# Grouped-query attention on one core: 120 score columns of every ninth chunk exponentiated on VectorE, PV three chunks behind, V spreads retimed

## The chip, the cores and the metric

One core of a Trainium2 chip. The metric is the device time of the whole program in microseconds, as a median of several executions. All executions used here count as fast ones; the granted TensorE clock is shown as 1.00 in the profiles, except where the text says otherwise.

## The reference

```python
# B, Hq, Hkv, Sq, Sk, D = 16, 32, 8, 288, 512, 128 ; bf16 ; q, k, v ~ 0.05 * normal
k = jnp.repeat(k, rep, axis=1)            # rep = 4 query heads per K/V head
v = jnp.repeat(v, rep, axis=1)
scores = jnp.einsum("bhqd,bhkd->bhqk", q, k) * D ** -0.5
p = softmax(scores, axis=-1)
return jnp.einsum("bhqk,bhkd->bhqd", p, v)
```

There are 16 x 8 = 128 groups (one K/V head each). A group has 4 x 288 = 1152 query rows, that is nine tiles of 128, and is worked through in three chunks of three tiles. So there are 384 chunks. A chunk has 512 keys x 384 rows of scores; laid out with keys on the partitions that is a 128 x 1536 tile.

## The kernel before

For each chunk n, TensorE makes the scores (six matmuls, 1536 columns), ScalarE takes the exponential of all 1536 columns in one instruction straight out of PSUM, TensorE multiplies by V (12 matmuls of 129 columns; the 129th column of V is one and gives the row sums), and VectorE takes the reciprocal of the sums and scales the result out of PSUM. GpSimd spreads V into a layout with room for the column of ones. No maximum is subtracted; a check of the sums at the end falls back to a general path that never runs here.

```python
def op_s(n):                                   # scores of chunk n
    waits = [have("k", g), have_q(g, i)]
    if n >= 2:
        waits.append(("s_e", n - 1))           # exponential n-2 is done: two score buffers
    for x, (c, j, r0, w) in enumerate(pieces): # 384,128,256,256,128,384 columns
        ... matmul(ps_s[:, n % 2, c:c + w], kt_sb[:, sl, j, gi, :], qg[:, r0:r0 + w])

def op_exp(n):                                 # ScalarE
    waits = [("s_s", n + 1)]
    if n >= NPT:                               # NPT = 4 probability buffers
        waits.insert(0, ("s_pv", n - NPT + 1))
    ... activation(pt_sb[:, n % NPT], ps_s[:, n % 2], Exp, scale=scale)

def op_pv(r):                                  # 12 matmuls into PSUM bank r % 2
    waits = [("s_vc", g + 1), ("s_e", r + 1)]
    if 2 <= r < NS - 1:
        waits.append(("s_ev", r - 1))          # eviction r-2 is done: two output banks

def op_vc(g):                                  # GpSimd spreads V of group g
    waits = [have("v", g)]                     # as soon as the load has landed
    if u >= NSLOT:
        waits.append(("s_pv", NC * (g - NSLOT * UG + 1)))
...
# TensorE's program                            # VectorE's program
for n in range(NS):                            # for r in range(NS - 1):
    op_s(n)                                    #     op_rc(r)   reciprocal
    if n >= LAG: op_pv(n - LAG)   # LAG = 2    #     op_ev(r)   eviction
```

Of the kernel before, what the change touches and what calls it, by code (L numbers as in the profile page):

```python
# [1 line left out]

# [118 lines left out]
    return {"pool": on_pool, "sp": on_sync, "pe": on_tensor, "dve": on_vector, "act": on_scalar}  # L121


def bass_standalone__gqa_softmax__near_ridge_kernel(
    nc: bass.Bass,
    q: bass.AP,
# [18 lines left out]
    assert COLS % CH == 0 and NT == NC * TPC and NJ * P == BANK  # L145
    scale = float(D) ** -0.5
    DV = D + 1
    VP = 160
    LAG = 2
    TW = TPC * P  # L150
    UG = 4
    NU = NG // UG
    NSLOT = 3
    NQ = 12
    NPT = 4
    WARM = 5
    AHEAD = 1.08
    NO = 12
    NS = NG * NC
# [10 lines left out]
    with ExitStack() as es:  # L170
# [14 lines left out]
            S("us_v%d" % i)  # L185
        for i in range(UG):
            S("s_k%d" % i)
        for name in ["s_v0", "s_v2", "s_s0", "s_kd0", "s_kd1", "s_id", "s_kp"]:
            S(name)
        for i in range(NQ):  # L190
            S("s_q%d" % i)
# [36 lines left out]
        st_sb = main.enter_context(nc.sbuf_tensor("st_sb", [P, 2, B], FP32))  # L228
        ck_sb = main.enter_context(nc.sbuf_tensor("ck_sb", [P, 3], FP32))
        bad_sb = main.enter_context(nc.sbuf_tensor("bad_sb", [P, 2, ALONE + 1], FP32))  # L230
        one_f = main.enter_context(nc.sbuf_tensor("one_f", [P, 1], FP32))
        z_sb = main.enter_context(nc.sbuf_tensor("z_sb", [P, BANK], BF16))
        dum = main.enter_context(nc.sbuf_tensor("dum", [P, 2], FP32))
# [15 lines left out]
        def emit(eng, waits, fn):  # L249
            waits = need(eng, waits)  # L250
            for (s, n) in waits[:-1]:
                eng.wait_ge(s, n)
            ins = fn()
            if waits:
                ins.wait_op(waits[-1][0], waits[-1][1], "sem-ge")
            return ins
# [95 lines left out]
        def op_s(n):  # L352
            eng = nc.tensor
            g, i = n // NC, n % NC
            sl, gi = (g // UG) % NSLOT, g % UG
            waits = [have("k", g), have_q(g, i)]
            if n >= 2:
                waits.append(("s_e", n - 1))
            qg = qt_sb[:, g % NQ, i * TPC:(i + 1) * TPC].rearrange("d t p -> d (t p)")
            for x, (c, j, r0, w) in enumerate(pieces):  # L360
                ins = emit(eng, waits if x == 0 else [], lambda: eng.matmul(  # L361
                    ps_s[:, n % 2, c:c + w], kt_sb[:, sl, j, gi, :], qg[:, r0:r0 + w], start=True, stop=True))
                if n == 0 and c + w == BANK:
                    ins.then_inc(sem["s_s0"], 1)
            ins.then_inc(sem["s_s"], 1)

        def outs(r):

# [4 lines left out]
        def op_pv(r):  # L373
            eng = nc.tensor
            g = r // NC
            sl, gi = (g // UG) % NSLOT, g % UG
            waits = [("s_vc", g + 1), ("s_e", r + 1)]
            if 2 <= r < NS - 1:
                waits.append(("s_ev", r - 1))


            for j in range(NJ):
                for a in range(TPC):
                    ins = emit(eng, waits if a == 0 and j == 0 else [], lambda: eng.matmul(  # L384
                        outs(r)[:, a, :], pt_sb[:, r % NPT, j, a * P:(a + 1) * P],
                        v_sb[:, sl, gi * NJ + j, 0:DV], start=(j == 0 and a == 0), stop=(j == NJ - 1),
                        skip_group_check=True))
            ins.then_inc(sem["s_pv"], 1)
# [13 lines left out]
        def op_exp(n):  # L402
            eng = nc.scalar
            waits = [("s_s", n + 1)]
            if n >= NPT:
                waits.insert(0, ("s_pv", n - NPT + 1))
            dst, src = pt_sb[:, n % NPT], ps_s[:, n % 2].rearrange("p (j r) -> p j r", r=TW)
            parts = [(dst.rearrange("p j r -> p (j r)"), ps_s[:, n % 2])]
            if n == 0:
                d, s = parts[0]  # L410
                emit(eng, [("s_s0", 1)], lambda: eng.activation(d[:, 0:BANK], s[:, 0:BANK], ACTF.Exp, scale=scale))  # L411
                parts = [(d[:, BANK:CH], s[:, BANK:CH])]
            if n == NS - 1:
                w = TW - P
                parts = [(dst[:, :, 0:w], src[:, :, 0:w]), (dst[:, :, w:TW], src[:, :, w:TW])]
            for (d, s) in parts:
                emit(eng, waits, lambda: eng.activation(d, s, ACTF.Exp, scale=scale)).then_inc(sem["s_e"], 1)  # L417


        def op_vc(g):  # L420
            eng = nc.gpsimd
            u, gi = g // UG, g % UG
            sl = u % NSLOT
            waits = [have("v", g)]
            if u >= NSLOT:
                waits.append(("s_pv", NC * (g - NSLOT * UG + 1)))
            emit(eng, waits, lambda: eng.tensor_copy(  # L427
                v_sb[:, sl, gi * NJ:(gi + 1) * NJ, 0:D], vd_sb[:, sl, gi].rearrange("p (j d) -> p j d", d=D))
            ).then_inc(sem["s_vc"], 1)
# [80 lines left out]
        @block.tensor  # L510
        def _(eng):
            op_warm(WARM, BANK, ps_o[:, 1])
            op_kt(0, range(NJ), 0)
            op_warm(6, P, ps_s[:, 1])
            for n in range(NS):
                if n == LAG:
                    op_kt(1, range(NJ), 1)
                    op_warm(4, P, ps_o[:, 0])
                op_s(n)
                if n >= LAG:  # L520
                    op_pv(n - LAG)
            for r in range(NS - LAG, NS - 1):
                op_pv(r)
            for a in range(TPC):
                op_pv_last(a)
            emit(eng, [("s_ev", NS - 1), ("s_bad", 2)], lambda: eng.matmul(  # L526
                ps_o[0:1, NS % 2, 0:ALONE + 1], one_f[:], bad_sb[:, 1, :], start=True, stop=True)
            ).then_inc(sem["s_bad"], 1)
            choose(eng, "pe")

        @block.scalar
        def _(eng):
            op_kd(eng, 0)
            emit(eng, [("s_one", 1)], lambda: eng.activation(dum[:, 1:2], dum[:, 0:1], ACTF.Exp))  # L534
            op_v(0, eng, 0, 2)
            op_kd(eng, 1)
            for n in range(NS):
                op_exp(n)
            op_ev_act()
            choose(eng, "act")  # L540
# [13 lines left out]
        def _(eng):  # L554
# [6 lines left out]
            w0 = NS - 1 - ALONE // TPC  # L561
            last = rl_sb[:, NG * NT - ALONE:NG * NT]
            for r in range(NS - 1):
                op_rc(r)
                op_ev(r)
                if r % per_b == per_b - 1 and r < NS - 1:
                    op_stat(r // per_b)
                if r == w0:
                    op_stat(B - 1)
                if r == w0 + 1:  # L570
                    emit(eng, [("s_stat", B)], lambda: eng.tensor_reduce(
                        ck_sb[:, 0:1], st_sb[:, 0, :], AX.X, ALU.max))
                    eng.tensor_reduce(ck_sb[:, 1:2], st_sb[:, 1, :], AX.X, ALU.min).then_inc(sem["s_stat"], 1)
                if r == w0 + 2:
                    op_over(ck_sb[:, 0:1], ck_sb[:, 1:2], ALONE, ALONE + 1, ("s_stat", B + 1), B + 2)
# [37 lines left out]
```

## Time and profile before

| | kernel before |
|---|---|
| median of 3 runs | 527.37 us (527.22 to 528.51) |
| span of the profiled run | 525.4 us |
| busy share TensorE, ScalarE, VectorE, GpSimd | 99, 99, 55, 14 % |
| score group to score group, first 30 chunks | 1.335 us |
| the same afterwards | 1.343 us |
| duration of one exponential as recorded | 1.46 us at the start, 1.76 us later |

The profile is of one execution. The views used in what follows: the page's busy times, the source view of one line (count, shortest/median/longest duration in ns, first and last start), the chain of waits (the work that ended last, in order of time), the table of waits, and the timeline. Two engines are shown as full, so the distance between the starts of one kind of instruction tells more than the busy share. The lines themselves are in the prediction below.

The *starts* of the first exponentials are 1.331 us apart but their *ends* 1.343, from the second chunk on: the recorded start of an instruction that sits behind another on ScalarE is not the start of its own work, and the growing duration is the difference. And TensorE's first score matmul of a chunk takes 0.163 us until the next in the first 30 chunks and 0.170 to 0.172 afterwards, which is the whole visible sign of its wait for ScalarE.

### The profile page before, as it was taken

The page shows a single profiled execution, that of the slowest core. Times are in us where ns is not written, and L with a number is a line of the kernel's source. Part 1 is how long each engine was busy: PE and PEld are TensorE (multiplying, and loading weights), DVE is VectorE, ACT ScalarE, POOL GpSimd, SP SyncE. Part 2 cuts the span into 40 slices and gives each one's busy share as a digit, 9 for nine tenths or more (in the row PEclk, how much of TensorE's full clock was granted, in tenths as well). Part 3 has the DMA queues.
Part 4 walks back from the last instruction along what each step waited for, and adds up shares of the span by engine and source line. Part 5 has one row for each costly group of instructions (what it writes and reads, how often), then busy time and mean ns, then how long its engine had stood idle before and what let it go on. Part 6 is the DMA issues. An engine that isn't in the chain of part 4 may idle for free.

```text
span 525.4 us, 16369 instructions
## 1 busy us (share of the span) xinstructions
PE 520.5 (99%) x6937; PEld 456.7 (87%) x6937; DVE 289.7 (55%) x812; ACT 517.9 (99%) x389; POOL 74.3 (14%) x135
## 2 busy tenths in 40 slices
PE   8999999999999999999999999999999999999997
PEld 6888888888888888888888888888888888888886
DVE  2555555555555555555555555555555555555555
ACT  6999999999999999999999999999999999999997
POOL 1210111111111101111111011110111101111000
PEclk9999999999999999999999999999999999999999
DMA  8999999899999999999999999999999999887112
GB/s 158 216 226 247 229 242 250 227 197 238 240 221 237 245 209 205 211 231 229 223 232 208 232 180 255 242 212 193 224 218 237 209 208 190 236 204 195 69 70 91
DMA packets 253143, 110.12 MB, mean 210 GB/s; under 512 B 219792, under 2 KB 236816, under 8 KB 253072
## 3 DMA queue, kind: packets, MB, share of 16 engines
q1 hardware_dynamic: 252512, 108.56, 97.3%
q8 instruction: 55, 0.90, 0.7%
q10 hardware_dynamic: 560, 0.52, 0.4%
q14 instruction: 16, 0.13, 0.1%
HBM read 17.04 MB, written 37.75 MB: 104 GB/s over the span
## 4 chain that ended last, share of the span: by engine, by line
PE 98%; DMA 1%; ACT 0%; DVE 0%; issue 0%
PE ps_o L384 50%; PE ps_s L361 48%; DMA qt_sb<-in_q_dram 1%; ACT pt_sb L417 0%; PE ps_s L395 0%; ACT pt_sb L411 0%; DVE o_sb L454 0%; PE ps_o L526 0%; DVE bad_sb L480 0%; DVE rl_sb L434 0%; DVE flag_i L580 0%; DVE bad_sb L477 0%
## 5 line engine op out<-in xcount | busy, mean ns | idle before, releaser
L417 ACT ACTIVATE pt_sb<-ps_s 128x1536 bf16<-128x1536 f32 (+1 forms) x385 | 515.6, 1746 | 0.0
L384 PE MATMUL ps_o<-v_sb,pt_sb 128*128 128x129 bf16 x4596 | 322.9, 220 | 0.0
L361 PE MATMUL ps_s<-qt_sb,kt_sb 128*128 128x384 bf16 (+2 forms) x2304 | 317.1, 274 | 0.7 <-DMA qt_sb<-in_q_dram 0.5
L384 PEld LDWEIGHTS ps_o<-v_sb,pt_sb 128*128 128x128 bf16 x4596 | 291.9, 98 | 24.8
L444 DVE TENSOR_TENSOR o_sb<-ps_o,rl_sb 128x384 bf16<-128x384 f32 x383 | 213.5, 558 | 13.3
L361 PEld LDWEIGHTS ps_s<-qt_sb,kt_sb 128*128 128x128 bf16 x2304 | 178.9, 98 | 37.5 <-DMA qt_sb<-in_q_dram 0.8
L434 DVE RECIPROCAL rl_sb<-ps_o 128x3 f32<-128x3 f32 x383 | 69.3, 181 | 213.9 <-PE ps_o L384 213.9
L427 POOL COPY v_sb<-vd_sb 128x512 bf16<-128x512 bf16 x128 | 73.3, 616 | 408.3 <-DMA vd_sb<-in_v_dram 383.7
L349 PE MATMUL ps_o<-z_sb 128*128 128x512 bf16 (+1 forms) x9 | 2.7, 447 | 1.3 <-DVE z_sb L555 1.3
L343 DVE COPY kt_sb<-ps_o 128x512 bf16<-128x512 bf16 x2 | 0.8, 425 | 5.3 <-PE ps_o L336 5.3
L411 ACT ACTIVATE pt_sb<-ps_s 128x512 bf16<-128x512 f32 x1 | 0.6, 598 | 2.9 <-PE ps_s L361 2.9
L470 DVE TENSOR_REDUCE st_sb<-rl_sb 128x1 f32<-128x72 f32 (+1 forms) x16 | 3.5, 216 | 0.0
L472 DVE TENSOR_REDUCE st_sb<-rl_sb 128x1 f32<-128x72 f32 (+1 forms) x16 | 3.5, 216 | 0.0
L349 PEld LDWEIGHTS ps_o<-z_sb 128*128 128x128 bf16 x9 | 0.9, 119 | 2.1 <-DVE z_sb L555 1.3
L534 ACT ACT_TABLE_LOAD x1 | 1.3, 1283 | 1.2 <-PEq L598 1.2
L336 PEld LDWEIGHTS ps_o<-ident,kd_sb 128*128 128x128 bf16 x8 | 0.7, 114 | 0.9 <-DMA kd_sb<-in_k_dram 0.8
L526 PE MATMUL ps_o<-bad_sb,one_f 128*1 128x25 f32 x2 | 0.2, 184 | 1.0 <-DVE bad_sb L480 1.0
L526 PEld LDWEIGHTS ps_o<-bad_sb,one_f 128*1 128x1 f32 x2 | 0.1, 80 | 1.2 <-DVE bad_sb L480 1.2
L461 ACT ACTIVATE o_sb<-ps_s,rl_sb 128x128 bf16<-128x128 f32 x1 | 0.4, 367 | 0.7 <-DVE rl_sb L434 0.7
L336 PE MATMUL ps_o<-ident,kd_sb 128*128 128x128 bf16 x8 | 1.0, 263 | 0.0
L395 PE MATMUL ps_s<-v_sb,pt_sb 128*128 128x129 bf16 x12 | 0.9, 222 | 0.0
L395 PEld LDWEIGHTS ps_s<-v_sb,pt_sb 128*128 128x128 bf16 x12 | 0.7, 98 | 0.2 <-ACT pt_sb L417 0.2
(22 smaller groups left out, 5.1 us busy)
## 6 DMA issues: line engine op xcount, KB each, us to landing
out_dram<-o_sb SPq DMA_DIRECT2D x127, 288.0 KB, 4.1
vd_sb<-in_v_dram SPq DMA_DIRECT2D x31, 512.0 KB, 5.5
qt_sb<-in_q_dram SPq DMA_TRANSPOSE x130, 5.0
kt_sb<-in_k_dram SPq DMA_TRANSPOSE x32, 5.3
out_dram<-o_sb SPq DMA_DIRECT2D x3, 96.0 KB, 1.6
kd_sb<-in_k_dram ACTq DMA_DIRECT2D x2, 128.0 KB, 3.2
vd_sb<-in_v_dram ACTq DMA_DIRECT2D x1, 256.0 KB, 3.7
vd_sb<-in_v_dram SPq DMA_DIRECT2D x1, 256.0 KB, 4.9
```

The lines of the kernel that those rows point to most:

```text
L336: ins = emit(eng, [("s_id", 2), ("s_kd%d" % g, 16)], lambda: eng.transpose(dst[:, x * P:(x + 1) * P], kd_sb[:, g, j * D:(j + 1) * D], iden ...
L349: emit(nc.tensor, [("s_z", 1)], lambda: nc.tensor.matmul(dst[:, 0:w], z_sb[:, 0:P], z_sb[:, 0:w], start=True, stop=True))
L361: ins = emit(eng, waits if x == 0 else [], lambda: eng.matmul(ps_s[:, n % 2, c:c + w], kt_sb[:, sl, j, gi, :], qg[:, r0:r0 + w], start=Tru ...
L384: ins = emit(eng, waits if a == 0 and j == 0 else [], lambda: eng.matmul(outs(r)[:, a, :], pt_sb[:, r % NPT, j, a * P:(a + 1) * P], v_sb[: ...
L395: ins = emit(eng, [("s_e", NS + (0 if a < TPC - 1 else 1))], lambda: eng.matmul(outs(NS - 1)[:, a, :], pt_sb[:, (NS - 1) % NPT, j, a * P:( ...
L417: emit(eng, waits, lambda: eng.activation(d, s, ACTF.Exp, scale=scale)).then_inc(sem["s_e"], 1)
L427: emit(eng, waits, lambda: eng.tensor_copy(v_sb[:, sl, gi * NJ:(gi + 1) * NJ, 0:D], vd_sb[:, sl, gi].rearrange("p (j d) -> p j d", d=D))). ...
L434: emit(eng, [("s_pv", r + 1)], lambda: eng.reciprocal(rl_sb[:, TPC * r:TPC * (r + 1)].unsqueeze(2), outs(r)[:, :, D:DV])).then_inc(sem["s_ ...
L444: emit(eng, waits, lambda: eng.tensor_tensor(out=o_sb[:, g % NO, t0:t0 + TPC, :], in0=outs(r)[:, :, 0:D], in1=rl_sb[:, TPC * r:TPC * (r + ...
L470: emit(eng, [("s_rc", e // TPC)], lambda: eng.tensor_reduce(st_sb[:, 0, b:b + 1], rl_sb[:, a:e], AX.X, ALU.max))
L472: eng.tensor_reduce(st_sb[:, 1, b:b + 1], rl_sb[:, a:e], AX.X, ALU.min).then_inc(sem["s_stat"], 1)
L534: emit(eng, [("s_one", 1)], lambda: eng.activation(dum[:, 1:2], dum[:, 0:1], ACTF.Exp))
```

## The change

The intent: ScalarE's exponential is a little slower per chunk than TensorE's matmuls, and VectorE has room. So in every ninth chunk the last 120 of the 1536 columns go to VectorE, which computes exp by bit operations: scale so that the exponent field comes out of a float-to-integer conversion, mask out mantissa and exponent, evaluate a quartic in the mantissa, multiply with the exponent part. That is eight VectorE instructions of 120 columns. They take longer than one chunk, so PV runs three chunks behind the scores instead of two. GpSimd's copies are triggered so that they miss the VectorE work. The diff is shortened, cuts are marked with "...", and some lines are joined or put as comments.

```diff
-    LAG = 2
+    LAG = 3
+    W = 120
+    EVERY = 9
-    NPT = 4
+    NPT = 6
+    FIRST_SHARED = 4
...
+                if shared(n) and c + w == CH:
+                    w -= W                                   # last score piece 264 instead of 384
...
+        def op_sy(n):                                        # the other 120, into the free end of PV's bank
+            emit(eng, [("s_ev", n - LAG - 1)], lambda: eng.matmul(
+                ps_o[:, (n - LAG) % 2, BANK - W:BANK], kt_sb[...], qt_sb[:, g % NQ, t, P - W:P], ...
...
+                    if a == TPC - 1 and j == NJ - 1 and shared(r):
+                        w_x = w_x + [("s_yp", nth(r))]       # last PV matmul waits for VectorE's columns
...
+            if shared(n):
+                parts = [(d[:, 0:CH - W], s[:, 0:CH - W]) for (d, s) in parts]
...
+        def shared(n):
+            return FIRST_SHARED <= n < NS - 6 and (n - FIRST_SHARED) % EVERY == 0
+        # op_y clamp, op_yb scale and shift, op_ym two masks, op_yu three polynomial steps, op_yp product
...
         def op_vc(g):
-            if u >= NSLOT:
-                waits.append(("s_pv", NC * (g - NSLOT * UG + 1)))
+            if g >= 2:
+                waits.append(("s_pv", NC * (g - 2) + 1))
...
             for r in range(NS - 1):
+                n = r + LAG
                 op_rc(r)
+                if shared(n): op_y(n)
+                if shared(n - 1): op_yu(n - 1, 1)
                 op_ev(r)
+                if shared(n): op_yb(n); op_ym(n); op_yu(n, 0)
+                if shared(n - 1): op_yu(n - 1, 2); op_yp(n - 1)
...
         # ScalarE's queue, first loads: K of group 0, then (after it has landed) K of group 1, then V
-            op_v(0, eng, 0, 2)
-            op_kd(eng, 1)
+            for (s, n) in need(eng, [("s_kd0", 16)]):
+                eng.wait_ge(s, n)
+            op_kd(eng, 1)
+            op_v(0, eng, 0, 2)
```

The transposes of group 1's K also move behind score group 2, and two more warming matmuls are issued.

More of the change, by code (lines that the diff above doesn't have):

```diff
@@ L1 @@
+import math
 from contextlib import ExitStack
@@ L121, in general_path @@
     return {"pool": on_pool, "sp": on_sync, "pe": on_tensor, "dve": on_vector, "act": on_scalar}
+LOG2E = math.log2(math.e)
+QUARTIC = (-0.039256332078737396, 0.7694109050129492, 0.36021799676460203, 0.1471865760029904)
+QUARTER_BITS = 0x3E800000
+LEAD_BITS = 0x3FDDBE69 & 0x7FFFFF
 def bass_standalone__gqa_softmax__near_ridge_kernel(
@@ L147, in bass_standalone__gqa_softmax__near_ridge_kernel @@
     DV = D + 1
+    Y_MAX = 126.0 / (scale * LOG2E)
+    Y_MUL, Y_ADD = scale * LOG2E * 2.0 ** 23, 128.0 * 2.0 ** 23
     VP = 160
-    LAG = 2
+    LAG = 3
+    W = 120
+    EVERY = 9
+    NB = 2
     TW = TPC * P
@@ L187, in bass_standalone__gqa_softmax__near_ridge_kernel @@
             S("s_k%d" % i)
-        for name in ["s_v0", "s_v2", "s_s0", "s_kd0", "s_kd1", "s_id", "s_kp"]:
+        for name in ["s_v0", "s_v2", "s_s0", "s_y", "s_yb", "s_ym", "s_yu", "s_yp", "s_kd0", "s_kd1", "s_id", "s_kp"]:
             S(name)
@@ L230, in bass_standalone__gqa_softmax__near_ridge_kernel @@
         bad_sb = main.enter_context(nc.sbuf_tensor("bad_sb", [P, 2, ALONE + 1], FP32))
+        y_sb = main.enter_context(nc.sbuf_tensor("y_sb", [P, NB, W], FP32))
+        t_sb = main.enter_context(nc.sbuf_tensor("t_sb", [P, NB, W], I32))
+        m_sb = main.enter_context(nc.sbuf_tensor("m_sb", [P, NB, W], I32))
+        e_sb = main.enter_context(nc.sbuf_tensor("e_sb", [P, NB, W], I32))
+        u_sb = main.enter_context(nc.sbuf_tensor("u_sb", [P, NB, 3, W], FP32))
         one_f = main.enter_context(nc.sbuf_tensor("one_f", [P, 1], FP32))
@@ L365, in op_s @@
             ins.then_inc(sem["s_s"], 1)
+        def op_sy(n):
+            eng = nc.tensor
+            g, t = n // NC, n % NC * TPC + TPC - 1
+            emit(eng, [("s_ev", n - LAG - 1)], lambda: eng.matmul(
+                ps_o[:, (n - LAG) % 2, BANK - W:BANK], kt_sb[:, (g // UG) % NSLOT, NJ - 1, g % UG, :],
+                qt_sb[:, g % NQ, t, P - W:P], start=True, stop=True))
         def outs(r):
@@ L383, in op_pv @@
                 for a in range(TPC):
-                    ins = emit(eng, waits if a == 0 and j == 0 else [], lambda: eng.matmul(
+                    w_x = waits if a == 0 and j == 0 else []
+                    if a == TPC - 1 and j == NJ - 1 and shared(r):
+                        w_x = w_x + [("s_yp", nth(r))]
+                    ins = emit(eng, w_x, lambda: eng.matmul(
                         outs(r)[:, a, :], pt_sb[:, r % NPT, j, a * P:(a + 1) * P],
@@ L417, in op_exp, with nth, op_y, op_yb @@
                 emit(eng, waits, lambda: eng.activation(d, s, ACTF.Exp, scale=scale)).then_inc(sem["s_e"], 1)
+        def shared(n):
+            return FIRST_SHARED <= n < NS - 6 and (n - FIRST_SHARED) % EVERY == 0
+        def nth(n):
+            return (n - FIRST_SHARED) // EVERY + 1
+        def op_y(n):
+            eng, b = nc.vector, nth(n) % NB
+            emit(eng, [("s_yb", nth(n) - NB), ("s_pv", n - LAG + 1)], lambda: eng.tensor_scalar(
+                out=y_sb[:, b], in0=ps_o[:, (n - LAG) % 2, BANK - W:BANK], scalar1=-Y_MAX, scalar2=Y_MAX,
+                op0=ALU.max, op1=ALU.min)).then_inc(sem["s_y"], 1)
+        def op_yb(n):
+            eng, b = nc.vector, nth(n) % NB
+            emit(eng, [("s_ym", 2 * (nth(n) - NB)), ("s_y", nth(n))], lambda: eng.tensor_scalar(
+                out=t_sb[:, b], in0=y_sb[:, b], scalar1=Y_MUL, scalar2=Y_ADD, op0=ALU.mult, op1=ALU.add)
+            ).then_inc(sem["s_yb"], 1)
+        def op_ym(n):
+            eng, b = nc.vector, nth(n) % NB
+            for x, (dst, mask, bits) in enumerate(((m_sb, 0x7FFFFF, QUARTER_BITS), (e_sb, 0x7F800000, LEAD_BITS))):
+                emit(eng, [("s_yp", nth(n) - NB), ("s_yb", nth(n))], lambda: eng.tensor_scalar(
+                    out=dst[:, b], in0=t_sb[:, b], scalar1=mask, scalar2=bits,
+                    op0=ALU.bitwise_and, op1=ALU.bitwise_or)).then_inc(sem["s_ym"], 1)
+        def op_yu(n, x):
+            eng, b = nc.vector, nth(n) % NB
+            m = m_sb[:, b].bitcast(FP32)
+            src = m if x == 0 else u_sb[:, b, x - 1]
+            emit(eng, [("s_ym", 2 * nth(n) - 1) if x == 0 else ("s_yu", 3 * nth(n) - 3 + x)],
+                 lambda: eng.scalar_tensor_tensor(
+                     out=u_sb[:, b, x], in0=src, scalar=QUARTIC[x], in1=m, op0=ALU.add, op1=ALU.mult)
+                 ).then_inc(sem["s_yu"], 1)
+        def op_yp(n):
+            eng, b = nc.vector, nth(n) % NB
+            emit(eng, [("s_pv", n - NPT + 1), ("s_ym", 2 * nth(n)), ("s_yu", 3 * nth(n))],
+                 lambda: eng.scalar_tensor_tensor(
+                     out=pt_sb[:, n % NPT, NJ - 1, TW - W:TW], in0=u_sb[:, b, 2], scalar=QUARTIC[3],
+                     in1=e_sb[:, b].bitcast(FP32), op0=ALU.add, op1=ALU.mult)).then_inc(sem["s_yp"], 1)
         def op_vc(g):
@@ L513, in _ @@
             op_kt(0, range(NJ), 0)
-            op_warm(6, P, ps_s[:, 1])
+            op_warm(8, P, ps_s[:, 1])
             for n in range(NS):
-                if n == LAG:
-                    op_kt(1, range(NJ), 1)
+                if n == 2:
                     op_warm(4, P, ps_o[:, 0])
                 op_s(n)
+                if shared(n):
+                    op_sy(n)
+                if n == 2:
+                    op_kt(1, range(NJ), 1)
                 if n >= LAG:
@@ L563, in _ @@
             for r in range(NS - 1):
+                n = r + LAG
                 op_rc(r)
+                if shared(n):
+                    op_y(n)
+                if shared(n - 1):
+                    op_yu(n - 1, 1)
                 op_ev(r)
+                if shared(n):
+                    op_yb(n)
+                    op_ym(n)
+                    op_yu(n, 0)
+                if shared(n - 1):
+                    op_yu(n - 1, 2)
+                    op_yp(n - 1)
                 if r % per_b == per_b - 1 and r < NS - 1:
```

## The prediction

> **What bounds the kernel now.** I read the page's busy times first, then the source view of the exponential, the chain of waits at two places, the table of waits, and the page's groups of VectorE last.
>
> ```profile
> PE 520.5 (99%) x6937; PEld 456.7 (87%) x6937; DVE 289.7 (55%) x812; ACT 517.9 (99%) x389; POOL 74.3 (14%) x135
> ```
>
> TensorE and ScalarE are both shown as full, so busy time alone cannot say which of them sets the pace. The source view of the exponential over the window 60 to 510 us can:
>
> ```profile
> L417 ACT ACTIVATE pt_sb<-ps_s x336: 1761/1762/1762, 59.2 to 509.2; 128x1536 bf16<-128x1536 f32 x168
> ```
>
> 336 exponentials start within 450.0 us, so one 1536-column chunk takes 450.0/335 = 1.343 us. The same view over 7.1 to 45 us shows something else:
>
> ```profile
> L417 ACT ACTIVATE pt_sb<-ps_s x30: 1017/1626/1754, 6.2 to 44.4; 128x1536 bf16<-128x1536 f32 x29, 128x1024 bf16<-128x1024 f32 x1
> ```
>
> Here the duration of one climbs steadily towards 1.76 us, and then stays there: ScalarE's queue is filling until something blocks. TensorE's side is the chain of waits, first over 20 to 44 us, then over 200 to 227 us (start, length, what):
>
> ```profile
> 20.99 0.66 PE ps_s L361 x6
> 21.64 0.68 PE ps_o L384 x12
> ...
> 43.68 0.33 PE ps_s L361 x3
> ```
>
> ```profile
> 200.84 0.66 PE ps_s L361 x6
> 201.51 0.68 PE ps_o L384 x12
> ...
> 226.37 0.67 PE ps_s L361 x6
> ```
>
> Score groups start 17 chunks apart at 20.99 and 43.68: 22.69/17 = 1.335 us per chunk. Later they start 19 chunks apart at 200.84 and 226.37: 25.53/19 = 1.344 us. So TensorE left alone needs 1.335 us, ScalarE 1.343 us. During about the first 30 chunks TensorE spends the lead that it had; after that its score group waits for the exponential two chunks before (two score buffers), and ScalarE sets the pace. This wait is some 8 ns a chunk, too short for the table of waits, which shows only VectorE waiting for TensorE:
>
> ```profile
> DVE rl_sb L434 <- PE ps_o L384: 213.9, 382, 1.4
> ```
>
> That is 0.56 us idle per chunk on VectorE, the room the change wants to use. The end confirms ScalarE: the last PV product waits for the last exponential (third line of the chain's end).
>
> ```profile
> 519.88 1.44 PE ps_o L384 x24
> 521.32 0.89 PE ps_s L395 x12
> 522.21 0.02 issue
> ```
>
> **What the Trainium skill says.** "TensorE: Matmul & The Clock Gate", section "Wait — 56ns, not 53.3ns?": a warm matmul costs its columns over 2.4 GHz plus about 2.5 ns. For this kernel that gives 1536/2.4 + 6 x 2.5 = 655 ns for scores and 12 x (129/2.4 + 2.5) = 675 ns for PV, 1.330 us; the trace has 1.335. It agrees, so TensorE has almost no idle left below 1.335.
> "ScalarE: Activation LUTs", section "What ACT_TABLE_LOAD costs": 0.833 ns per element, 186 ns per instruction with immediates, some 93 ns of it overlapped. That would be 1280 + 93 = 1.373 us; the trace has 1.343, so here the fixed part is 63 ns. The slope agrees: the two pieces of the last exponential (1024 and 512 columns) end near 521.25 and 521.74, and 0.49 = 512 x 0.833 + 0.06.
> "Perfetto Trace Analysis", section "Optimizing Scalar/DVE Operations": the write-acknowledge half of a VectorE instruction overlaps with the next. The timeline agrees: two independent reductions of 218 ns start 0.14 us apart.
>
> ```profile
> 40.40 0.22 DVE L470 TENSOR_REDUCE st_sb<-rl_sb 128x1 f32<-128x72 f32 x1
> 40.54 0.22 DVE L472 TENSOR_REDUCE st_sb<-rl_sb 128x1 f32<-128x72 f32 x1
> ```
>
> "SBUF — State Buffer", section "Who interferes with whom": a VectorE instruction in a two-port mode, or with two SBUF inputs, and a GpSimd instruction that reads SBUF block one another. No VectorE bulk instruction of the kernel before is of that kind (its evictions read PSUM and one SBUF operand), so its trace shows nothing of it; the new ones are.
>
> **The change part by part.**
> *ScalarE.* Chunks 4, 13, ... 373 are shared: (373 - 4)/9 + 1 = 42 chunks. Each gives up 120 columns: 120 x 0.833 = 100 ns. Over nine chunks ScalarE needs 9 x 1.3433 - 0.100 = 11.990 us, or 1.332 us a chunk, just below TensorE's 1.335. The size is chosen to get below it by the least. Between two shared chunks ScalarE falls behind by 8 x 8 = 66 ns. At the start the lead is some 0.3 us (exponential 1 ends about 8.5, score group 3 starts at 8.81), so TensorE should not meet ScalarE again.
> *TensorE.* A shared chunk's last score piece is 264 columns, and the 120 are a matmul of their own into the free end of PV's output bank: one more instruction, +2.5 ns; 42 of them 0.1 us. The three new waits (for PV's old bank, and for VectorE's part before the last PV matmul) cost nothing if they are met beforehand.
> *VectorE.* Durations from the groups of the page: fixed cost about 0.15 us, about 1.04 ns a column (384 columns 558 ns, 256 columns 424 ns; SCALAR_TENSOR_TENSOR of 1 column 160 ns, of 24 185 ns). Estimates for 120 columns from these: clamp out of PSUM 275 ns, each of three TENSOR_SCALAR 220 to 270, each of four SCALAR_TENSOR_TENSOR 285. A dependent one starts 35 ns after the end of the one before (reciprocal to eviction), an independent one 84 ns before it. Let t = 0 be the reciprocal of PV(n-3). First iteration: reciprocal to 0.18, clamp to 0.37, eviction to 0.85 (0.77 before), scale and shift to about 1.0, the two masks to about 1.45, first polynomial step to 1.57 to 1.72. The next reciprocal is due at 1.335 and so starts 0.15 to 0.3 late. Second iteration: its eviction ends at 2.4 to 2.5, last polynomial step and product at 2.9 to 3.0. Third: everything done by 3.6 to 3.7, before 4.0, when VectorE is on time again. The deadlines: PV(n) of the second next chunk needs a bank some 1.8 us after the matching reciprocal was due, so the second eviction may end at about 3.0 and the third at 4.3; the last PV matmul of chunk n needs VectorE's columns at about 3.7. Slack: 0.5, 0.6 and 0.7 us. Without PV three behind (one chunk earlier: 2.35) the columns would be late, which is what that part is for.
> *GpSimd.* 128 copies of 616 ns each stay. They now start after PV(3(g-2)), that is one chunk before and two chunks after a chain of VectorE begins, six chunks ahead of need. The first is over by then; the second can touch the last product.
> *The ends.* At the start PV(0) moves behind score group 3, and the transposes of group 1 take its place; score group 3 stays near 8.9 (8.81 before). Its cost is that TensorE has one PV (0.68 us) more to do from there. At the finish three PV groups, 2.0 us, follow the last score group, longer than the last exponential's 1.6 us, so the last wait goes too. The K block now loads ahead of V and of the second K block; that may bring score group 0 in 0.1 to 0.3 us earlier.
>
> *The sum.* Before, from score group 3 (8.81) TensorE had 381 x 0.655 + 383 x 0.680 = 510.0 us of work and issued its last PV at about 522.03: 3.2 us of waiting, the eight ns of 350 chunks (2.9 us) and 0.3 at the end. After: start 8.9, work 381 x 0.655 + 384 x 0.680 + 0.1 = 510.8, so 519.7, 2.35 us earlier. With 0.2 us for the earlier loads: 527.37 - 2.55 = **524.8 us**.
>
> **The rivals.**
> 1. *VectorE becomes the wait.* If nothing overlaps and every instruction is a little longer, the chain ends near 3.7 to 3.9 us instead of 3.0, and PV(n) or the eviction after it stalls 50 to 100 ns, 42 times: 2 to 4 us, the whole gain. For it: seven dependent steps, each with a fixed 0.15 us. Against: the two reductions do overlap, and 0.5 us of slack remains. Time then 526.5 to 529.
> 2. *GpSimd blocks VectorE's two-input instructions.* A 616 ns copy just ahead of the last product would shift it from 3.0 to about 3.5: still before 3.7. Against: the copies were retimed for this. If it loses, 10 to 50 ns per shared chunk: at most 2 us, 526 to 527.
> 3. *V arrives or is spread too late, or transfers bind.* The DMA row is near 9 for most of the run. Against: the queue itself waits for TensorE and VectorE, and in the table of waits no matmul of the steady part waits for a load. It would cost under 1 us.
> 4. *TensorE's 1.335 hides a dependence on ScalarE*, so that more is gained. Against: 1.335 is within 5 ns of the work by columns. At most 1 us more.
>
> **Range and chances.** Nothing here can reach 2% (10.5 us): TensorE's own work alone is some 98% of the time before, and a loss would need 250 ns of stall in every shared chunk. Range 524.0 to 526.6, lopsided for rivals 1 and 2. Faster by over 2%: 0.005; within 2%: 0.985; slower by over 2%: 0.01.
>
> **What would show it right or wrong.** Right: score groups 1.335 to 1.336 us apart over the whole run; exponentials of 1416 columns 42 times; durations of the exponential that stop climbing towards 1.76 us and stay between 1.45 and about 1.6; no wait of TensorE for ScalarE at the end. Wrong: chunks over 1.34 us next to shared ones with TensorE waiting for VectorE's product or eviction (rival 1), the same with VectorE instructions far longer than 285 ns during a GpSimd copy (rival 2), or score groups still 1.343 apart, in which case ScalarE was not the bound.

## The result

| | before | changed |
|---|---|---|
| median | 527.30 us (4 runs, 527.12 to 528.51) | 525.22 us (4 runs, 525.11 to 526.08) |
| ratio, 95% interval | | 0.9959 (0.9941 to 0.9978) |
| span of the profiled run | 525.4 us | 523.5 us |

A ratio is the mean time of one kernel's fast runs over the mean of the other's of the same rounds, so it is not quite the ratio of the medians. The changed kernel is 0.4% faster, and clear of noise by its interval.

The page's busy times of the changed kernel:

```profile
PE 517.6 (99%) x6981; PEld 459.0 (88%) x6981; DVE 339.9 (65%) x1148; ACT 515.1 (98%) x389; POOL 79.6 (15%) x135
```

As before, TensorE and ScalarE look equally full; VectorE went from 55 to 65%. The source view of the exponential over 60 to 510 us tells the difference:

```profile
L453 ACT ACTIVATE pt_sb<-ps_s x338: 1402/1461/1495, 59.3 to 509.3; 128x1536 bf16<-128x1536 f32 x150, 128x1416 bf16<-128x1416 f32 x19
```

338 instead of 336 exponentials in the same 450.0 us, and the duration of one stays between 1.40 and 1.50 us. ScalarE still falls behind by some 8 ns a chunk between two shared chunks (the recorded duration climbs from 1.44 to 1.49 us), but each shared chunk lets it catch up, so the backlog no longer reaches the 1.76 us at which TensorE had to wait. (The shape counts at the end of the line are of a sample.) The chain of waits over 200 to 227 us has the score groups:

```profile
201.51 0.66 PE ps_s L384 x6
202.16 0.68 PE ps_o L418 x12
...
226.88 0.16 PE ps_s L384
```

Nineteen chunks from 201.51 to 226.88 us are 1.335 us each (1.344 before). In the trace every distance after the start is 1.335 us, but 42 of 1.337 to 1.338, one per shared chunk. Added up over the 378 chunks after score group 5, TensorE lost 0.10 us against 1.335 us a chunk, where the kernel before lost 2.94.

VectorE's chain for one shared chunk, in the timeline (start, length):

```profile
132.12 0.18 DVE L512 RECIPROCAL rl_sb<-ps_o 128x3 f32<-128x3 f32 x1 [0.56 <-PE ps_o L418]
132.21 0.25 DVE L464 TENSOR_SCALAR y_sb<-ps_o 128x120 f32<-128x120 f32 x1
132.38 0.55 DVE L522 TENSOR_TENSOR o_sb<-ps_o,rl_sb 128x384 bf16<-128x384 f32 x1
132.85 0.21 DVE L470 TENSOR_SCALAR t_sb<-y_sb 128x120 int32<-128x120 f32 x1
133.09 0.22 DVE L477 TENSOR_SCALAR m_sb<-t_sb 128x120 int32<-128x120 int32 x1
133.23 0.22 DVE L477 TENSOR_SCALAR e_sb<-t_sb 128x120 int32<-128x120 int32 x1
133.36 0.28 DVE L486 SCALAR_TENSOR_TENSOR u_sb<-m_sb 128x120 f32<-128x120 f32 x1
133.56 0.17 DVE L512 RECIPROCAL rl_sb<-ps_o 128x3 f32<-128x3 f32 x1
133.67 0.28 DVE L486 SCALAR_TENSOR_TENSOR u_sb<-u_sb,m_sb 128x120 f32<-128x120 f32 x1
133.87 0.55 DVE L522 TENSOR_TENSOR o_sb<-ps_o,rl_sb 128x384 bf16<-128x384 f32 x1
134.34 0.27 DVE L486 SCALAR_TENSOR_TENSOR u_sb<-u_sb,m_sb 128x120 f32<-128x120 f32 x1
134.65 0.28 DVE L493 SCALAR_TENSOR_TENSOR pt_sb<-u_sb,e_sb 128x120 bf16<-128x120 f32 x1
```

From the reciprocal at 132.12 to the end of the product at 134.93 it takes 2.81 us. Independent neighbours overlap (the clamp starts 0.09 us after the reciprocal, which lasts 0.18), dependent ones do not. The last PV matmul of the chunk starts 0.93 us after the product ends, in the median of the 42; nothing waits for VectorE there.

The table of waits has VectorE's idle time and the only wait of TensorE for VectorE in the attention work (the others are in the warming matmuls at the start and in the check of the sums at the end):

```profile
DVE rl_sb L512 <- PE ps_o L418: 160.8, 297, 1.9
...
PEld ps_o L418 <- DVE o_sb L522: 0.4, 1, 0.4
```

That one wait is at the finish. The timeline of TensorE there:

```profile
516.47 0.82 PE L384 MATMUL ps_s<-qt_sb,kt_sb 128*128 128x384 bf16 x6
517.13 1.52 PE L418 MATMUL ps_o<-v_sb,pt_sb 128*128 128x129 bf16 x24
518.84 0.85 PE L418 MATMUL ps_o<-v_sb,pt_sb 128*128 128x129 bf16 x12 [0.19 <-DVE o_sb L522]
519.53 0.84 PE L429 MATMUL ps_s<-v_sb,pt_sb 128*128 128x129 bf16 x12
```

After the last score group the PV groups come 0.68 us apart instead of 1.335. Group 382 needs the output bank of group 380, whose eviction ends only at 518.78 us; the matmul that could have come at 518.49 starts at 518.84. And the start, in the same view:

```profile
7.16 0.81 PE L384 MATMUL ps_s<-qt_sb,kt_sb 128*128 128x384 bf16 x6 [0.58 <-DMA qt_sb<-in_q_dram]
7.81 0.39 PE L357 MATMUL ps_o<-ident,kd_sb 128*128 128x128 bf16 x4
9.07 0.81 PE L384 MATMUL ps_s<-qt_sb,kt_sb 128*128 128x384 bf16 x6 [0.87 <-DMA qt_sb<-in_q_dram]
```

Score group 3 starts at 9.07 us, held by the load of group 1's Q; in the kernel before it started at 8.81.

### The profile page after: what moved, and what is told of

Read it like the earlier page. It is cut to its first block, busy times and chain, and to the rows that moved or that the text cites. A ratio compares the mean times of both kernels' runs of the same rounds, so it can differ in the third digit from the quotient of the medians.

```text
span 523.5 us, 16876 instructions
## 1 busy us (share of the span) xinstructions
PE 517.6 (99%) x6981; PEld 459.0 (88%) x6981; DVE 339.9 (65%) x1148; ACT 515.1 (98%) x389; POOL 79.6 (15%) x135
## 4 chain that ended last, share of the span: by engine, by line
PE 97%; DMA 1%; SPq 1%; DVE 0%; issue 0%
PE ps_o L418 50%; PE ps_s L384 47%; DMA qt_sb<-in_q_dram 1%; SPq L315 1%; PE ps_o L394 0%; DVE o_sb L522 0%; DVE rl_sb L512 0%; DVE o_sb L532 0%; PE ps_o L607 0%; DVE bad_sb L558 0%; DVE flag_i L675 0%; DVE bad_sb L555 0%
## 5 line engine op out<-in xcount | busy, mean ns | idle before, releaser
L453 ACT ACTIVATE pt_sb<-ps_s 128x1536 bf16<-128x1536 f32 (+2 forms) x385 | 512.8, 1455 | 0.6 <-PE ps_s L384 0.5
L384 PE MATMUL ps_s<-qt_sb,kt_sb 128*128 128x128 bf16 (+3 forms) x2304 | 312.2, 272 | 1.5 <-DMA qt_sb<-in_q_dram 1.4
L384 PEld LDWEIGHTS ps_s<-qt_sb,kt_sb 128*128 128x128 bf16 x2304 | 193.4, 98 | 35.6 <-issue 1.0
L486 DVE SCALAR_TENSOR_TENSOR u_sb<-u_sb,m_sb 128x120 f32<-128x120 f32 x84 | 23.4, 278 | 0.0
L493 DVE SCALAR_TENSOR_TENSOR pt_sb<-u_sb,e_sb 128x120 bf16<-128x120 f32 x42 | 12.2, 290 | 1.4
L486 DVE SCALAR_TENSOR_TENSOR u_sb<-m_sb 128x120 f32<-128x120 f32 x42 | 11.6, 277 | 0.0
L464 DVE TENSOR_SCALAR y_sb<-ps_o 128x120 f32<-128x120 f32 x42 | 10.6, 253 | 0.0
L477 DVE TENSOR_SCALAR m_sb<-t_sb 128x120 int32<-128x120 int32 x42 | 9.4, 223 | 1.4
L477 DVE TENSOR_SCALAR e_sb<-t_sb 128x120 int32<-128x120 int32 x42 | 9.5, 226 | 0.0
L394 PE MATMUL ps_o<-qt_sb,kt_sb 128*128 128x120 bf16 x42 | 9.1, 216 | 0.0
```

What stands on the lines that cost most here:

```text
L384: ins = emit(eng, waits if x == 0 else [], lambda: eng.matmul(ps_s[:, n % 2, c:c + w], kt_sb[:, sl, j, gi, :], qg[:, r0:r0 + w], start=Tru ...
L394: emit(eng, [("s_ev", n - LAG - 1)], lambda: eng.matmul(ps_o[:, (n - LAG) % 2, BANK - W:BANK], kt_sb[:, (g // UG) % NSLOT, NJ - 1, g % UG, :],
L453: emit(eng, waits, lambda: eng.activation(d, s, ACTF.Exp, scale=scale)).then_inc(sem["s_e"], 1)
L464: emit(eng, [("s_yb", nth(n) - NB), ("s_pv", n - LAG + 1)], lambda: eng.tensor_scalar(out=y_sb[:, b], in0=ps_o[:, (n - LAG) % 2, BANK - W: ...
L477: emit(eng, [("s_yp", nth(n) - NB), ("s_yb", nth(n))], lambda: eng.tensor_scalar(out=dst[:, b], in0=t_sb[:, b], scalar1=mask, scalar2=bits ...
L486: lambda: eng.scalar_tensor_tensor(out=u_sb[:, b, x], in0=src, scalar=QUARTIC[x], in1=m, op0=ALU.add, op1=ALU.mult)
```

## The experiments

The theory to be tested: ScalarE's 1.343 us a chunk was the bound; 42 x 120 columns bring it to 1.332, just under TensorE's 1.335; PV three behind and the retimed V spreads only keep VectorE's chain from being waited for. The rivals: the third chunk of distance alone removes the wait; ScalarE is still the bound; VectorE or GpSimd cost something, too. Each edit is against the changed kernel. All ten new kernels gave correct results.

### No column shared

```diff
-            return FIRST_SHARED <= n < NS - 6 and (n - FIRST_SHARED) % EVERY == 0
+            return False
```

> The changed kernel with no chunk shared: PV three behind, six probability buffers, the load order and the retimed V spreads all stay, but ScalarE keeps all 1536 columns of every chunk. Theory (ScalarE's 1.343 us a chunk was the bound, and only the columns given away lift it): score groups go back to 1.343 us apart once the first lead is spent, exponentials last 1.76 us again, time 527.3 to 528.3 us, at or slightly above the kernel before. Rival (PV one chunk further behind is what removed the wait, the columns hardly matter): time stays near 525.2 us and score groups 1.335 apart.

Measured: 528.22 us (528.14 to 528.33, 5 runs), ratio to before 1.0007 (0.9989 to 1.0025). Source view of the exponential over 60 to 510 us:

```profile
L453 ACT ACTIVATE pt_sb<-ps_s x336: 1744/1762/1762, 59.5 to 509.5; 128x1536 bf16<-128x1536 f32 x168
```

336 exponentials in 450.0 us, 1.76 us each: the picture of the kernel before. So the distance of PV is worth nothing by itself. The gain is the columns'.

### Half the dose

```diff
-    EVERY = 9
+    EVERY = 18
```

> Half the dose: every eighteenth chunk shared, 21 in all. Theory: ScalarE then needs 1.3433 - 0.100/18 = 1.3378 us a chunk, 2.6 ns over TensorE's 1.335; once a lead of some 0.15 to 0.3 us is spent (60 to 115 chunks) score groups are 1.338 us apart on average, so about 0.8 us are lost: 525.8 to 526.3 us. Rival (a share of any size breaks the coupling): 525.2 us.

Measured: 526.22 us (526.04 to 526.50, 5 runs), inside the theory's range.

```profile
L453 ACT ACTIVATE pt_sb<-ps_s x337: 1525/1703/1762, 59.4 to 508.8; 128x1536 bf16<-128x1536 f32 x150, 128x1416 bf16<-128x1416 f32 x19
```

The exponentials climb to 1.76 us between shared chunks and fall back at them. TensorE's loss against 1.335 us a chunk is 0.82 us, where no sharing has 2.84 and every ninth chunk 0.10.

### One and a half times the dose

```diff
-    EVERY = 9
+    EVERY = 6
```

> One and a half times the dose: every sixth chunk, 63 in all. Theory: TensorE is the bound already at every ninth, so nothing more is gained; 21 more split score pieces cost 2.5 ns each, 0.05 us: 525.2 to 525.5 us, score groups 1.335 us apart. Rival (ScalarE still sets the pace): it would need 1.3266 us a chunk and 2 us more would be gained, 523.1 us.

Measured: 525.37 us (525.14 to 525.75, 5 runs).

```profile
L453 ACT ACTIVATE pt_sb<-ps_s x338: 1378/1451/1471, 59.2 to 509.2; 128x1536 bf16<-128x1536 f32 x112, 128x1416 bf16<-128x1416 f32 x57
```

338 exponentials in 450.0 us, as with every ninth chunk. Sharing every ninth chunk takes 100/9 = 11 ns a chunk off ScalarE, every sixth 17 ns, and the further 6 ns bought nothing: TensorE is the bound. The 21 further splits show as 0.05 us more lost (0.15 against 0.10).

### V spreads as before

```diff
-            if g >= 2:
-                waits.append(("s_pv", NC * (g - 2) + 1))
+            if u >= NSLOT:
+                waits.append(("s_pv", NC * (g - NSLOT * UG + 1)))
```

> The changed kernel with the V spreads timed as before the change: bursts of four copies as soon as a V load lands. Theory on GpSimd (the two-input and two-port instructions of VectorE and the copies block one another; about a third of the 32 bursts fall on one of the 42 chains, a burst of 2.4 us against 0.93 us of slack): some of those instructions last 0.6 us instead of 0.22 to 0.28, some chains end late and TensorE waits; 526 to 530 us. Rival (the slack of 0.93 us swallows it, the retiming was not needed): 525.2 us with long instructions but no wait of TensorE.

Measured: 526.52 us (526.18 to 529.54, 6 runs). All six lie above the kernel that shares every sixth chunk, measured in the same rounds (525.14 to 525.75); two of them, 528.12 and 529.54, are outliers whose profile was not taken. The timeline of a chain that a burst of four copies met, first GpSimd, then VectorE:

```profile
108.51 2.29 POOL L505 COPY v_sb<-vd_sb 128x512 bf16<-128x512 bf16 x4 [13.31 <-DMA vd_sb<-in_v_dram]
```

```profile
109.09 0.67 DVE L470 TENSOR_SCALAR t_sb<-y_sb 128x120 int32<-128x120 f32 x1
109.79 0.52 DVE L477 TENSOR_SCALAR m_sb<-t_sb 128x120 int32<-128x120 int32 x1
110.23 0.64 DVE L477 TENSOR_SCALAR e_sb<-t_sb 128x120 int32<-128x120 int32 x1
110.79 0.27 DVE L486 SCALAR_TENSOR_TENSOR u_sb<-m_sb 128x120 f32<-128x120 f32 x1
```

Three instructions that normally last 0.21 to 0.22 us take 0.52 to 0.67 us each while copies run; the fourth, after the burst, is back at 0.27. This is what the Trainium skill says in "SBUF — State Buffer", section "Who interferes with whom": a VectorE instruction in a two-port mode or with two SBUF inputs and a GpSimd instruction that reads SBUF exclude one another. Instructions of one and of two SBUF inputs were stretched here, 14 in 6 of the 42 chains (13 to between 0.52 and 0.69 us, one to 0.39). That the one-input ones run in a two-port mode is inferred; the trace does not name modes. It does hold a control: in 7 chains a copy lay beside the clamp, which reads PSUM, and the clamp lasted 0.25 us as always; the evictions beside copies kept their 0.55 to 0.56 us. In three of the six chains TensorE was late: by 0.42 us at 111.9 and 0.10 us at 173.4, where an eviction came too late for its bank, and by 0.12 us at 245.0, where the last PV matmul waited for VectorE's columns. In all, the profiled run (526.18 us) lost 0.69 us more than the changed kernel's (525.22) in the steady part, and its score group 3 began 0.26 us later; together 0.95 of the 0.96 us. So in this trace the retiming is worth about 0.7 us, not the almost 5 us that the upper end of the expectation allowed for: most chains either miss the bursts or have the slack.

### PV two behind

```diff
-    LAG = 3
+    LAG = 2
```

> The changed kernel with PV two chunks behind again instead of three; everything else stays. Theory (the chain of VectorE ends 0.93 us before the last PV matmul of its chunk needs it; one chunk less takes 1.335 us away): 42 times the last PV matmul waits 0.40 to 0.50 us, 17 to 21 us in all, so 542 to 546 us, and the table of waits shows TensorE waiting 42 times for VectorE's product. Rival (the third chunk is only for comfort, the chain would be hurried or the wait hidden behind the next score group): under 527 us.

Measured: 556.28 us (555.75 to 556.47, 4 runs), ratio 1.0537. The direction was right, the size was not. Table of waits, then the timeline of TensorE and of VectorE around one such wait:

```profile
PEld ps_o L418 <- DVE pt_sb L493: 31.9, 42, 0.8
```

```profile
128.76 0.79 PE L418 MATMUL ps_o<-v_sb,pt_sb 128*128 128x129 bf16 x11
130.13 0.23 PE L418 MATMUL ps_o<-v_sb,pt_sb 128*128 128x129 bf16 x1 [0.59 <-DVE pt_sb L493]
```

```profile
128.53 0.57 DVE L486 SCALAR_TENSOR_TENSOR u_sb<-u_sb,m_sb 128x120 f32<-128x120 f32 x1
```

The last of the 12 PV matmuls starts 0.81 us after the one before it instead of 0.057, a wait of 0.75 us, 42 times. The second polynomial step lasts 0.57 us instead of 0.28, here as in 36 of the 42 chains: a V copy from 128.33 to 128.97 us stands beside it. With PV two behind, the chain begins one chunk later relative to PV, and the copies, which follow PV, hit every chain. I had not carried the coupling of the two parts through.

### PV two behind, V spreads one chunk later

```diff
-    LAG = 3
+    LAG = 2
-                waits.append(("s_pv", NC * (g - 2) + 1))
+                waits.append(("s_pv", NC * (g - 2) + 2))
```

> PV two behind again, and each V spread one chunk later, so that it misses the chain of VectorE as it does in the changed kernel. In the run before, every chain met a V copy: its second polynomial step lasted 0.57 us instead of 0.28, and the last PV matmul waited 0.75 us instead of the 0.40 to 0.50 expected. If that copy is the difference, the wait falls to about 0.46 us, the time to 543 to 546 us, and no polynomial step lasts over 0.3 us. If the chain is later for another reason, the time stays near 556 us.

Measured: 546.29 us (546.16 to 546.46, 4 runs), 0.3 us above the range. Source view of the polynomial steps:

```profile
L486 DVE SCALAR_TENSOR_TENSOR u_sb<-u_sb,m_sb x84: 251/274/285, 13.6 to 528.4; 128x120 f32<-128x120 f32 x84
```

No step is long any more, and the wait of the last PV matmul is 0.46 us in the median (0.52 from its neighbour, less 0.06). Against 1.335 us, 34 of the shared chunks lost 0.47 to 0.48 us and 8 lost 0.68 to 0.84, together 21.8 us. Of those 8, five have the two statistics reductions of VectorE (218 to 222 ns each) within the chain and one a V copy beside its scale-and-shift step (0.58 us instead of 0.21); in the other two an eviction within the chain starts 0.23 us later than in the rest, and why stays open. So of the 31 us that PV two behind costs, some 20 are the missing chunk and 10 the copies. From 0.93 us of slack in the changed kernel to 0.46 us of wait here are 1.39 us: one chunk of 1.335 and 0.05 more.

### The changed kernel again, and its finish

> The changed kernel once more, as the one to compare the ends with on the same chip: 525.2 us, score group 3 near 9.07 us, PV group 382 starting near 518.84 us after a wait of 0.35 us for an eviction.

Measured: 525.42 us (525.40 to 525.56, 5 runs); score group 3 at 9.18 us, PV group 382 after 0.35 us of wait at 518.95.

```diff
+            if r == NS - 2:
+                return ps_s[:, (NS - 2) % 2, 0:TPC * DV].rearrange("p (a e) -> p a e", e=DV)
             if r == NS - 1:
-                return ps_s[:, (NS - 2) % 2].rearrange("p (a e) -> p a e", e=BANK)[:, :, 0:DV]
+                st = 2 * DV
+                return ps_s[:, (NS - 2) % 2, BANK:BANK + TPC * st].rearrange("p (a e) -> p a e", e=st)[:, :, 0:DV]
-            if 2 <= r < NS - 1:
+            if 2 <= r < NS - 2:
                 waits.append(("s_ev", r - 1))
```

> The changed kernel with PV group 382 put into the score buffer that is free by then, so that it need not wait for the eviction of group 380; the last group goes into the other two banks of that buffer. If that wait of 0.35 us is the loss at the finish, the time falls by 0.3 to 0.4 us against the changed kernel on the same chip, to about 524.9 us. Rival: the finish is bound by VectorE's three evictions in a row, and less than 0.15 us is gained.

Measured: median 525.00 us (524.65 to 529.00, 6 runs), 0.42 us under the changed kernel on the same chip, and the wait at the finish is gone from the trace. The profile happens to be that of the 529.00 us run, and it shows where this outlier comes from. Its table by stretch for 3 to 16 us, and TensorE's timeline:

```profile
3.00:16.00 13.00, 10.35 (x78) 7.92 (x77) 1.59 (x4) 6.67 (x6) 1.78 (x3) 0.74 0.99 194
```

```profile
8.71 1.44 PE L384 MATMUL ps_s<-qt_sb,kt_sb 128*128 128x384 bf16 x6 [2.08 <-DMA qt_sb<-in_q_dram]
```

The third piece of Q landed at 8.6 us instead of 7.0; TensorE stood for 2.1 us and then worked at a granted clock that is 0.74 on average over this stretch (the third number from the end of the row; 1.00 in the changed kernel's profile). Score group 4 begins at 13.67 us instead of 10.40, and group 5 at 15.87 instead of 11.74. From there on the two traces are alike, 1.335 us a chunk. So in this run the start cost the 4 us, not the steady part. Whether the outliers of the other kernels have the same cause was not seen, since they were not profiled; that of 529.54 us in the run with the V spreads as before has a mean granted clock of 0.996, which would fit.

### The first loads in the old order

```diff
-            for (s, n) in need(eng, [("s_kd0", 16)]):
-                eng.wait_ge(s, n)
-            op_kd(eng, 1)
             op_v(0, eng, 0, 2)
+            op_kd(eng, 1)
-            op_warm(8, P, ps_s[:, 1])
+            op_warm(6, P, ps_s[:, 1])
```

> The changed kernel with the first loads in the order of the kernel before (V of groups 0 and 1, then K of group 1, at once) and 6 warming matmuls instead of 8. If the load of the first Q block after the first group is what holds score group 3 (9.04 us in the changed kernel, 8.70 in the kernel before), and it lands earlier with the old order, score group 3 starts near 8.8 us and the time is 0.2 to 0.3 us shorter: 525.0 us. If the new order helps, as the prediction had it, the time is 0.1 to 0.3 us longer: 525.4 us.

Measured: median 526.24 us (525.25 to 526.77, 6 runs). My first expectation is refuted, and the second one is exceeded: the median is 0.8 us longer than the changed kernel's on the same chip. In the profiled run (526.77 us) score group 0 began at 5.52 us instead of 4.62 and score group 3 at 10.54 instead of 9.07. (The expectation's 9.04 us is the weight load of that group; for the kernel before the trace has 8.78, not 8.70.) TensorE's timeline shows that not all of the difference is loads:

```profile
5.52 2.74 PE L384 MATMUL ps_s<-qt_sb,kt_sb 128*128 128x384 bf16 x12 [0.71 <-DMA qt_sb<-in_q_dram]
```

The same twelve matmuls took 1.74 us in the changed kernel's trace. In these traces the first matmuls follow one another at about half the later pace (a warming matmul of 128 columns every 107 ns, later every 56). The pace changed at 4.54 us in the changed kernel's trace, at 5.97 in that of the V spreads as before, whose start is the same program, and only at 9.41 here; the clock column, which has no record before that moment, shows 1.00 for 5.5 to 9.4 us of this run all the same. The best of the six (525.25) is as good as the changed kernel, and the kernel before, with this order and 6 warming matmuls, began score group 3 at 8.81 us. So the edit makes the start less steady; whether by the load order, the two warming matmuls or the moment of that change of pace was not separated.

### Both ends mended

The finish of above, and the first group's Q in two loads instead of three:

```diff
-            c0, c1 = i * TPC, (i + 1) * TPC
+            c0, c1 = (0, TPC) if i == 0 else (TPC, NT)
-                return ("s_qp%d" % i, 16)
+                return ("s_qp%d" % min(i, 1), 16)
-        first = [lambda i=i: op_q0(i) for i in range(NC)]
+        first = [lambda i=i: op_q0(i) for i in range(2)]
```

> The finish of the run before, and the first group's Q loaded in two pieces (3 and 6 tiles) instead of three, which frees 1.3 us of the queue's issue time ahead of group 1's Q. If that load holds score group 3, it lands near 7.8 us instead of 8.96 and score group 3 starts near 8.6 us instead of 9.07: another 0.3 to 0.5 us less, about 524.5 us. If score group 1 now waits longer for its larger piece, the gain is eaten: 524.9 us.

Measured: 524.75 us (524.56 to 524.87, 5 runs), ratio to before 0.9940 (0.9925 to 0.9955). The time is in the range, but the reason is not the one given: group 1's Q was issued at 3.52 us instead of 4.77 and still landed at 8.93, and score group 3 began at 9.07. The issue time of the queue was not what held it; in this trace the whole gain over the changed kernel is the finish (0.35 us of the span).

> The kernel with both ends mended once more, as the one to compare the next with on the same chip: 524.7 us again, against 527.5 us before.

Measured: 524.70 us (524.64 to 524.89, 6 runs). In this profiled run group 1's Q landed at 8.70 and score group 3 began at 8.83. The 11 runs of this kernel lie within 0.33 us. It is the fastest kernel, 0.6% under the kernel before and 0.7 us under the changed one.

```diff
-            op_v(0, eng, 0, 2)                 # ScalarE's queue; the rest of the edit as above
-        first += [lambda: op_q(1), lambda: op_k(0, 2), ...
+        first += [lambda: op_q(1), lambda: op_v(0, None, 0, 2), lambda: op_k(0, 2), ...
```

> The kernel with both ends mended, with V of groups 0 and 1 loaded behind Q of group 1 instead of ahead of it. If the load of Q of group 1 (landed at 8.93 us whether issued at 4.77 or at 3.52) is held by the bytes queued ahead of it, it lands near 8 us, score group 3 starts at 8.85 us instead of 9.07, and 0.2 us are gained: 524.5 us. If V then comes too late for PV group 0 (near 9.7 us), as much or more is lost.

Measured: 525.01 us (524.77 to 525.07, 6 runs), 0.3 us worse. The first half came out: behind fewer bytes, group 1's Q landed at 7.45 us. But score group 3 began only at 8.94 (group 0's second piece had landed later, and the transposes with it), and V, landed at 9.18, held PV group 0 until 9.90 us. So this move only moved the wait, from Q to V.

## Why the prediction was right

Predicted 524.8 us in 524.0 to 526.6, measured 525.22.

* **The bound.** Right. The pace went from 1.343 to 1.335 us, as two numbers of the trace before had said, and the doses of 0, 21, 42 and 63 shared chunks gave losses of 2.84, 0.82, 0.10 and 0.15 us: a bound that hands over to another one at the dose chosen.
* **ScalarE's saving.** Right: a shared exponential ends 1.243 us after the one before it, where others take 1.343. The 120 columns are 100 ns. The exponential after a shared one ends 1.374 us after it: there ScalarE has caught up and waits some 0.03 us for TensorE, which is the spare time of this dose.
* **TensorE's addition.** Right: 2.5 ns a shared chunk, 0.10 us in all.
* **VectorE's chain.** Right in its steps: 2.81 us against 2.9 to 3.0, the clamp 253 ns against 275, the other TENSOR_SCALARs 211 to 225 against 220 to 270, the polynomial steps and the product some 279 against 285. The slack came out at 0.93 us against 0.7; the last PV matmul came 3.75 us after the reciprocal (3.7 predicted), so the difference is the product's earlier end. Without overlap of independent neighbours rival 1 would have been near; it did not come about.
* **GpSimd (rival 2).** The mechanism is there, but in the changed kernel only the very first chain met it (one mask lasted 631 ns and the product 572, beside copies that had waited for V at 13.0 and 14.6 us); its slack shrank to 0.23 us and no matmul waited.
* **Rivals 3 and 4.** Neither came about. In the table of waits TensorE waits for loads only at the start, and every distance of the steady part is 1.335 to 1.338 us; relieving ScalarE further (63 shared chunks) did not bring TensorE under 1.335.
* **The start: wrong by 0.37 us.** The step "score group 3 stays near 8.9" and the credit of "0.2 us for the earlier loads" put score group 3 at 8.7; it came at 9.07 in the profiled run. Score group 0 did come 0.62 us earlier, but group 1's Q landed at 8.94 instead of 8.67, and the gain in front of it evaporated. The run with the old order took longer still (526.24 us), but for reasons that were not separated.
* **The finish: wrong by 0.35 us.** The step "so the last wait goes too" overlooked that three PV groups in a row come faster than VectorE can evict into two banks. One wait went, another took its place; the experiment on the finish shows it worth 0.42 us. (The wait of the kernel before that the prediction speaks of is real, but the three lines it shows do not name it; the table of waits does, 0.2 us of TensorE's weight load behind the exponential.)
* **The sum.** 0.37 + 0.35 are 0.7 us of the span: predicted last PV matmul at 519.5, measured 520.15. The time missed by only 0.4 us by luck, because I took the gain off the median of 527.37 us, while the profiled run that I worked it out from took 527.04.

## What to carry to other kernels

When two engines are both shown as full, compare the distance of their starts in a stretch where one still has a lead with a later stretch: the two numbers are the two bounds, and the smaller one is what relieving the other can reach; give away just as much as gets there. A chain on a third engine is free as long as it ends before its reader needs it, so count its dependent steps at full length and its independent ones with overlap, and if it does not, let the reader run further behind, with the buffers that this takes (a faster chain was not tried). Parts of a change that are timed against each other (here PV's distance and GpSimd's copies) have to be moved together, and what happens at both ends, where the rhythm of the middle does not hold, has to be worked out by itself.

## What the Trainium skill lacked or had wrong

* "ScalarE: Activation LUTs", section "What ACT_TABLE_LOAD costs": its 186 ns an instruction less 93 ns of overlap would make 1.373 us of a 1536-column exponential; read from PSUM back to back it takes 1.343 us, a fixed part of 63 ns. The page does not say for which memory its figures hold; "Perfetto Trace Analysis", section "Optimizing Scalar/DVE Operations", has about 51 ns for ScalarE on PSUM, which is nearer. The slope of 0.833 ns per element holds (1416 columns: 1.243 us).
* The same section has nothing on how a saturated ScalarE looks in a trace: starts 1.331 to 1.335 us apart, ends 1.343, and a recorded duration that climbs from 1.457 to 1.762 us over some 30 instructions without the work of one changing.
* "SBUF — State Buffer", section "Who interferes with whom": agrees, and the runs add the size. A 128x120 instruction of VectorE lasted 0.52 to 0.69 us instead of 0.21 to 0.28 beside a copy of some 0.62 us, and a burst of four copies stretched three instructions in a row. Those that read PSUM were not stretched (the clamp: 0.25 us, 7 times).
